# Projecting one row's queries with the weights as the moving operand

## The chip, the cores and the metric

The kernel runs on one core of a Trainium2 chip. Its time is the device time of one execution in microseconds. Before the change three runs gave 1077.71, 1078.51 and 1079.8 us; the median, 1078.51, is what a change is held against. A separate execution was taken with the hardware profiler; all durations below come from it.

## The reference

Two layers, each of an attention block "A" and an MLP block "B", are applied twice to eight rows x of 448 numbers, with the same weights and caches both times. The first A is called pass 0 below, the second pass 1.

```
def A(x):                       # B=8, Sq=1, D=448, Hq=16, Hkv=8, Sk=4096, Dh=256
    q = (x @ wq) in 16 heads of 256
    k, v = k_cache, v_cache, each head used by 2 heads of q
    p = softmax(q k / 16)
    return (p v, heads side by side) @ wo
def B(x):
    h  = gelu(layernorm(x) @ w1)
    x1 = x + shifted(h) @ w2    # shifts by 1 and 2 along a sequence of length 1
    return x1 + gelu(layernorm(x1) @ w3) @ w4

x = x + A(layernorm(x)); x = x + B(layernorm(x))
x = x + A(layernorm(x)); x = x + B(layernorm(x))
```

The sequence has one position, so all four shifts leave zeros and the product with w2 is zero: w1 and w2 drop out of the work. What is large are the two caches: 8 elements x 8 heads x 4096 x 256 in bf16, 134 MB each, and both passes need both.

## The kernel before, in words

**Staging.** One SBUF tile, `places`, holds 15 pieces of 1 MB. A piece is a quarter of the K or the V of two heads of one element. All weights stay in SBUF: `wq_sb` (the first 384 rows of wq as three blocks of 128 rows, the last 64 rows as two halves stacked in one block), `w3_sb`, `wo_sb`, `w4_sb`. For each element, 12 of its 32 pieces are kept from pass 0 to pass 1, so they are loaded once; one more is put aside in PSUM (`away`, `back`), and a quarter of another.

**Order.** The whole order of the work is made when the program is built. `block` and `first_kept` write a list of items (task, K or V, quarter); a task is (pass, element, pair of head pairs). The main loop (L985) walks the list. A K item is turned by DVE (`transpose_k`, L803) and multiplied with the queries (`scores`, L818) into the PSUM bank `sc`, from which ACT takes exponentials (`exps`, L827) into `p_n`. A V item is multiplied with the probabilities by `pv` (L871), 16 products of 256 columns, each with 8 columns of `ptw` as weights, four of them going to the four row groups of the bank `o`. Behind each item `emit_loads` issues on SP's queue the loads for which places have come free; a load waits until the last reader of its place is done. SP's queue thus follows the pace at which items are consumed.

**Generators.** Work that is not tied to an item (finishing an element's heads, the output projection, the MLP, the next queries) is written as generators. `step` (L930) advances them by one `yield` at a time between items, or, for V items of the set `narrow`, between the two halves of an item (`between` in `pv`, at y == 8). A yield of 0 in such a calm stretch runs straight on to the next yield; a yield of 2 or 3 may skip the next turn.

**The chain of one element** (`chain`, L522) runs in pass 0 once the second half of an element's heads is there: `half` (scales the outputs and turns them to columns; it copies a bank of `o` to `o_sb`, and `locked` keeps two such halves apart), the output projection by `wo_sb` (`add_cols`), the MLP (`mlp`: `norm`, w3, gelu, w4), and the queries for pass 1: `project_q(b, 1, ...)`. All of it stands among the V items of `narrow`, which are loaded in halves of 512 KB (`halved`, L793). At the end `give_q` spreads the queries with four products (`spread_q`, L353) and four DVE copies into `qbd`, which the scores of pass 1 use as weights.

**The projection of one element** (L323 to L344). For each of 32 blocks of 128 columns of wq there are four products, one for each block of rows: the 128x128 block of wq is loaded as weights, and x, one column broadcast to 32 (`wide`, L167), streams past. The result comes out in columns, as the queries are wanted, in a region of the bank `misc`. A yield stands behind 32 products, so there are four groups of 32, each followed by half a V item or a whole one. DVE then copies 128x32 values to `qT`.

The eight elements' projections stand at about 172, 300, 429, 558, 675, 784, 893 and 1002 us of the profiled span.

Of the kernel before, what the change touches and what calls it, by code (L numbers as in the profile page):

```python
# [8 lines left out]
FP32 = mybir.dt.float32  # L9
BF16 = mybir.dt.bfloat16  # L10
# [7 lines left out]
def kernel(  # L18
# [27 lines left out]
    nc = tc.nc  # L46
# [3 lines left out]
    Dh = A_k_cache.shape[3]  # L50
    HD = A_wq.shape[1]
    Hq = HD // Dh
# [5 lines left out]
    HC = F // 128  # L58
# [11 lines left out]
    consts = ctx.enter_context(tc.tile_pool(name="consts", bufs=1))  # L70
    work = ctx.enter_context(tc.tile_pool(name="work", bufs=2))
    chn = ctx.enter_context(tc.tile_pool(name="chn", bufs=1))
# [10 lines left out]
    MID = Bn // 2  # L83
# [5 lines left out]
    ident = spare[1][:, 0:256].bitcast(FP32)  # L89
# [1 line left out]
    identb = consts.tile([128, 128], BF16, name="identb")  # L91
    nc.vector.tensor_copy(identb[:], ident)

    usel = consts.tile([128, 4], FP32, name="usel")
    for u in range(2):
        nc.vector.tensor_reduce(
            usel[:, 2 * u : 2 * u + 2],
# [10 lines left out]
        ALU.add,  # L108
    )

    ptz = consts.tile([128, 264], BF16, name="ptw")
    nc.vector.memset(ptz[:], 0.0)
    ptw = ptz[:, 0:256].rearrange("p (r n w) -> p r n w", r=2, w=8)
    psv_t = consts.tile([128, NP * 128], BF16, name="psv")
    psv = [
# [1 line left out]
        for k in range(NP)  # L117
    ]

    misc = psum.tile([128, 512], FP32, name="misc")  # L120
    ot_bank = misc[:, 256:288]
    sc = psum.tile([128, 512], FP32, name="sc")
# [7 lines left out]
    def room_ps(what, nb):  # L130

        at, n = {"y": (288, 8), "st": (296, 2), "h": (298, HC), "q": (288, NB2)}[what]
        if nb == 1:
            return misc[:, at : at + n]
        if nb < Bn:
            at = {"y": 352, "st": 384, "h": 400}[what]
            return misc[:, at : at + n * nb]
        at, n = {"y": (0, 8), "st": (64, 2), "h": (80, HC), "q": (256, NB2)}[what]
        return store[0][:, at : at + n * nb]
# [39 lines left out]
    def xbs(nb):  # L179
        return xb[1] if nb == 1 else xb[Bn][:, :, :nb]  # L180
# [10 lines left out]
    wq_sb = split_tile(HD, "wq_sb")  # L191
# [205 lines left out]
    def mlp_hidden(b0, nb):  # L397

        yield from norm(xT[:, :, b0 : b0 + nb], nb, True)
        h_ps = room_ps("h", nb)  # L400
        for c in range(HC):
            for fc in range(4):
                w, xi = wblk(w3_sb, F, c, fc)
                if nb == 1:
                    wide(h_ps[:, c : c + 1], w, xbs(1)[:, xi, :], fc == 0, fc == 3)
                    continue
                nc.tensor.matmul(
                    h_ps[:, c * nb : c * nb + nb],
                    w,
                    xbs(nb)[:, xi, :],  # L410
                    start=(fc == 0),
                    stop=(fc == 3),
                )
            if c % 7 == 6:
                yield 0 if c == HC - 1 else None
        g_t = chn.tile([128, HC * MID], FP32, tag="g")
        hh = g_t[:, 0 : HC * nb]
        g0 = g_t[:, HC : 2 * HC] if nb == 1 else misc[:, 456 : 456 + HC * nb]
        if nb == 1:
            HT_t = chn.tile([128, HC, 1], BF16, tag="HT")  # L420
            HT = HT_t[:]
        else:
            HT = HTw[:, :, b0 : b0 + nb]

        nc.vector.tensor_scalar_mul(hh, h_ps, 0.5)
        nc.vector.scalar_tensor_tensor(g0, hh, 4 * 0.044715, hh, ALU.mult, ALU.mult)
        nc.vector.scalar_tensor_tensor(g0, g0, 1.0, hh, ALU.add, ALU.mult)
        nc.scalar.activation(g0, g0, ACT.Tanh, scale=2 * 0.7978845608028654)
        yield 0
        nc.vector.scalar_tensor_tensor(  # L430
            HT,
            g0.rearrange("p (c b) -> p c b", b=nb),
            1.0,
            hh.rearrange("p (c b) -> p c b", b=nb),
            ALU.add,
            ALU.mult,
        )
        yield 2
        return HT

    def mlp(b0, nb):
        HT = yield from mlp_hidden(b0, nb)
        yield from out_cols(lambda c: HT[:, c, :], w4_sb, HC, b0, nb, 2)

    def z_cols(zall, gps):

        np_ = len(gps)
        zm = chn.tile([128, 4, np_], FP32, tag=f"zm{np_}")
        zs_t = chn.tile([128, 2], FP32, tag="zs")
        zs = zs_t[:, 0:np_]  # L450
        nc.vector.tensor_add(
            zs, zall[:, 0, gps[0] : gps[-1] + 1], zall[:, 1, gps[0] : gps[-1] + 1]
        )
        nc.vector.tensor_tensor(
            zm[:],
            zs.unsqueeze(1).to_broadcast([128, 4, np_]),
            usel[:].unsqueeze(2).to_broadcast([128, 4, np_]),
            ALU.mult,
        )
        yield  # L460
        z_ps = misc[:, 392 : 392 + 4 * np_].rearrange("p (n g) -> p n g", n=4)
        nc.tensor.matmul(z_ps, ones, zm[:], start=True, stop=True)  # L462
        yield 0
        rz = chn.tile([128, 4, np_], FP32, tag=f"rz{np_}")
        nc.vector.reciprocal(rz[:], z_ps)  # L465
        return rz
# [6 lines left out]
                OT[:, j, h0 : h0 + 2], o_ps[:, j, h0 : h0 + 2], rz[:, 2 * u : 2 * u + 2, 0]  # L473
            )

    def half(o_ps, zall, gps, OT, ready):

        while locked:
            yield
        locked.append(gps)  # L480
        rz = yield from z_cols(zall, gps)

        g8, n8 = gps[0] // 2, 4 * len(gps)
        R_t = chn.tile([128, 8], FP32, tag="R")
        R = R_t[:, 0:n8]
        f0 = 4 * (gps[0] % 2)
        nc.vector.tensor_mul(
            R.rearrange("p (g n) -> p g n", n=4),
            rz[:].rearrange("p n g -> p g n"),
            fold[:, f0 : f0 + n8].rearrange("p (g n) -> p g n", n=4),  # L490
        )
        while not ready():
            yield
        o_sb = chn.tile([128, Dh], FP32, tag="o_sb")
        nc.scalar.copy(o_sb[:], o_ps)  # L495
        yield
        nc.vector.memset(o_ps, 0.0)  # L497
        free_o.append(o_ps)
        ot_ps = ot_bank[:, 16 * g8 : 16 * g8 + 2 * n8].rearrange("p (j h) -> p j h", j=2)
        for j in range(2):  # L500
            nc.tensor.matmul(  # L501
                ot_ps[:, j], o_sb[:].rearrange("p (i j) -> p j i", j=2)[:, j], R, start=True, stop=True
            )
        yield 0
        nc.vector.tensor_copy(OT, ot_ps)  # L505
        locked.pop()
        yield

    locked = []
    free_o = list(o_banks)  # L510

    def first_half(b, st, ready):
# [6 lines left out]
        xs = xT[:, :, b : b + 1]  # L519
        nc.vector.tensor_add(xs, xs, y_room(1)[:, 0])  # L520

    def chain(b, st, ready):  # L522
        OT = work.tile([128, 2, Hq // 2, 1], BF16, tag="OTb", bufs=1)
        yield from half(st["o", 1], st["z"], [2, 3], OT[:, :, :, 0], ready)
        yield from add_cols(
            y_room(1)[:, 1],
            lambda i: OT[:, i % 2, i // 2 - Hq // 2],
            wo_sb,
            range(NB2 // 2, NB2),
            2,  # L530
        )
        xs = xT[:, :, b : b + 1]
        nc.vector.tensor_add(xs, xs, y_room(1)[:, 1])
        yield from mlp(b, 1)
        qT = chn.tile([128, NB2], BF16, tag="qT2", bufs=2)
        yield from project_q(b, 1, qT[:].unsqueeze(2))
        state[1, b] = {"qT": qT}
        give_q((1, b))

# [381 lines left out]
    gens, pairs_done, p_of = [], {}, {}  # L921
# [63 lines left out]
    for idx, it in enumerate(items):  # L985
# [7 lines left out]
        n, kv, c = it  # L993
        ps, b, gp = tasks[n]
# [4 lines left out]
        p = where[(b, gp), (kv, c)] if kept_now else where[it]  # L999
# [3 lines left out]
        if kv == 0:  # L1003
# [6 lines left out]
            st = state[ps, b]  # L1010
# [13 lines left out]
            x = c - c % 2  # L1024
# [11 lines left out]
                    scores(two[0], x, qbd, gp, between=turn)  # L1036
                    scores(two[1], x + 1, qbd, gp)
            if c == 1:
                p_n = work.tile([128, 4, 32, 4], BF16, tag="p_sb", bufs=1)
                p_of[n] = p_n  # L1040
            if c % 2 == 1:
                exps(p_of[n], st["z"], gp, c // 2)
                if kept_now and c == 3:
# [4 lines left out]
        else:  # L1048
            st = state[ps, b]
# [28 lines left out]
            else:  # L1078
# [9 lines left out]
                if c == 0 and (alone_now or pairs_done.get((ps, b), 0) % 2 == 1):  # L1088
# [5 lines left out]
                    if ps == 0:  # L1094
                        g = (first_half if done == 2 else chain)(b, st, ready)
# [100 lines left out]
```

## Time and profile before

| | |
|---|---|
| median of three runs | 1078.51 us |
| profiled execution | 1078.9 us |
| its span | 1077.1 us |
| mean granted TensorE clock | 0.663 |
| read from HBM | 436.28 MB |
| rate over the span | 405 GB/s |
| products by wq in the eight chains (L170) | 1024, mean 184 ns each, 33.5 us busy in all |
| their weight loads | 1024, 30.0 us busy |
| halves of V (512 KB loads) | 202, median 7.4 us from issue to landing |

A line of a group names the source line, engine and operation, then the output tile, the inputs, the shapes and the count. "PE" is TensorE's matmuls, "PEld" its weight loads, which run beside matmuls; "SPq" is the queue on which SP issues loads. In a timeline a line stands for consecutive instructions of one kind: start and length in us, and in brackets how long the engine had been idle before, and what ended that. The windows view gives, for a stretch, the busy time of each engine with the number of instructions, the granted clock, the busy share of the 16 DMA engines and the rate in GB/s. The chain of waits goes back from the last instruction to whatever released each step.

### The profile page before, as it was taken

The numbers are of one execution on the slowest core, as the hardware profiler recorded it, in microseconds if no ns is written. First come the engines' busy times: TensorE is split into PE (matmuls) and PEld (weight loads), VectorE is DVE, ScalarE is ACT, GpSimd is POOL, SyncE is SP. The second block draws the span as 40 slices with busy tenths as digits, with TensorE's granted clock in tenths as the row PEclk, the third lists the DMA queues.
The fourth block names the chain that finished last, engine by engine and source line by source line (L and its number), as shares of the span: only waits on it lengthen the run. The fifth ranks groups of instructions, "written<-read, shape, count | busy, mean of one in ns | idle before, by whom it ended". The sixth has DMA issues, their size and how long they took to land.

```text
span 1077.1 us, 29813 instructions
## 1 busy us (share of the span) xinstructions
PE 631.0 (59%) x13292; PEld 399.4 (37%) x13292; DVE 610.7 (57%) x1266; ACT 162.0 (15%) x612; POOL 16.4 (2%) x27
## 2 busy tenths in 40 slices
PE   3244457644765447654586547754775467756775
PEld 2122225422443224432254324532453245433554
DVE  4357841677426872368724773297439743875371
ACT  0001111111111111111111111111111111111110
POOL 0000000000000000000000000000000000000000
PEclk9998568755686556865567656755585567656765
DMA  9999999999999999999999999999999999999994
GB/s 359 394 426 423 426 412 402 424 424 423 403 404 425 426 422 389 417 425 424 420 385 417 424 424 401 397 426 426 409 399 424 424 410 402 425 424 389 409 419 176
DMA packets 69200, 438.22 MB, mean 407 GB/s; under 512 B 7368, under 2 KB 11344, under 8 KB 38736
## 3 DMA queue, kind: packets, MB, share of 16 engines
q1 hardware_dynamic: 68880, 435.94, 98.7%
q8 instruction: 104, 1.70, 0.6%
q10 hardware_dynamic: 192, 0.38, 0.1%
q14 instruction: 24, 0.20, 0.0%
HBM read 436.28 MB, written 0.01 MB: 405 GB/s over the span
## 4 chain that ended last, share of the span: by engine, by line
DMA 64%; PE 18%; DVE 11%; SPq 3%; issue 2%; ACT 2%; POOL 0%; DVEq 0%; ACTq 0%
DMA places<-in_A_v_cache_dram 35%; DMA places<-in_A_k_cache_dram 28%; DVE places L803 7%; PE o L871 6%; PE sc L818 6%; PE misc L170 3%; SPq L189 2%; PE misc L501 1%; SPq L790 1%; ACT p_n L827 1%; DMA wq_sb<-in_A_wq_dram 1%; DVE places L845 1%; DVE store L838 1%; DVE qbd L357 0%; PE misc L854 0%
## 5 line engine op out<-in xcount | busy, mean ns | idle before, releaser
L803 DVE STREAM_TRANSPOSE places<-places 128x512 uint32<-128x512 uint32 (+1 forms) x576 | 457.9, 857 | 127.0 <-DMA places<-in_A_k_cache_dram 125.5
L818 PE MATMUL sc<-places,qbd 128*8 128x256 bf16 (+1 forms) x4896 | 239.8, 343 | 247.8 <-DVE places L803 241.5
L871 PE MATMUL o<-places,ptw 128*8 128x256 bf16 x3968 | 232.4, 360 | 130.7 <-DMA places<-in_A_v_cache_dram 106.1
L818 PEld LDWEIGHTS <-qbd 128*8 128x8 bf16 x4896 | 125.9, 101 | 325.1 <-DVE places L803 147.1
L871 PEld LDWEIGHTS <-ptw 128*8 128x8 bf16 x3968 | 97.9, 99 | 195.5 <-issue 122.1
L827 ACT ACTIVATE p_n<-sc 128x256 bf16<-128x256 f32 x128 | 95.2, 743 | 382.1 <-PE sc L818 382.1
L981 ACT COPY ptw<-psv 128x32 bf16<-128x32 bf16 x248 | 52.6, 227 | 196.4 <-PE o L871 190.5
L861 ACT CAST psv<-misc 128x128 bf16<-128x128 f32 x64 | 17.0, 266 | 237.0 <-PE misc L854 237.0
L465 DVE RECIPROCAL rz<-misc 128x8 f32<-128x8 f32 (+1 forms) x35 | 6.6, 190 | 70.6 <-PE misc L462 70.6
L357 DVE CAST qbd<-misc 32x64 bf16<-32x64 f32 x104 | 22.4, 215 | 29.9 <-PE misc L353 28.9
L170 PEld LDWEIGHTS <-wq_sb 128*128 128x128 bf16 x1024 | 30.0, 101 | 15.2 <-issue 14.7
L170 PE MATMUL misc<-xb,wq_sb 128*128 128x32 bf16 x1024 | 33.5, 184 | 3.6 <-issue 2.9
L501 PE MATMUL misc<-R_t,o_sb 128*128 128x8 f32 (+1 forms) x132 | 26.7, 311 | 13.4 <-ACT o_sb L495 7.1
L170 PEld LDWEIGHTS <-wo_sb 128*128 128x128 bf16 x1024 | 30.1, 102 | 10.9 <-issue 10.7
L170 PE MATMUL misc<-OT,wo_sb 128*128 128x32 bf16 x1024 | 32.7, 185 | 1.9 <-DVE OT L505 1.7
L827 ACT ACTIVATION_READ_ACCUMULATOR p_n<-sc 128x1 f32 x128 | 33.8, 264 | 0.0
L501 PEld LDWEIGHTS misc<-R_t,o_sb 128*128 128x128 f32 x132 | 23.8, 252 | 23.5 <-ACT o_sb L495 13.6
L170 PEld LDWEIGHTS <-w_sb 128*128 128x128 bf16 x896 | 27.3, 103 | 13.8 <-issue 13.2
L343 DVE CAST qT<-misc 128x32 bf16<-128x32 f32 x8 | 1.5, 192 | 50.8 <-PE misc L170 50.8
L269 POOL TENSOR_TENSOR t<-t,nhalf 128x2 f32<-128x2 f32 (+2 forms) x20 | 14.0, 705 | 1048.4 <-DVE t L290 1048.4
L497 DVE MEMSET o<- 128x256 f32 x33 | 9.0, 272 | 34.2 <-PE o L871 31.2
L854 PEld LDWEIGHTS <-p_n 128*128 128x128 bf16 x256 | 11.8, 105 | 31.7 <-issue 20.4
(111 smaller groups left out, 312.3 us busy)
## 6 DMA issues: line engine op xcount, KB each, us to landing
places<-in_A_k_cache_dram SPq DMA_DIRECT2D x65, 2048.0 KB, 19.1
places<-in_A_v_cache_dram SPq DMA_DIRECT2D x107, 1024.0 KB, 21.0
places<-in_A_v_cache_dram SPq DMA_DIRECT2D x202, 512.0 KB, 7.4
places<-in_A_k_cache_dram SPq DMA_DIRECT2D x62, 1024.0 KB, 13.2
places<-in_A_v_cache_dram SPq DMA_DIRECT2D x8, 768.0 KB, 14.3
wo_sb<-in_A_wo_dram SPq DMA_DIRECT2D x1, 3584.0 KB, 27.1
wq_sb<-in_A_wq_dram SPq DMA_DIRECT2D x3, 1024.0 KB, 9.9
w_sb<-in_B_w_dram SPq DMA_DIRECT2D x1, 1568.0 KB
```

The costliest lines, as they stand in the source:

```text
L170: nc.tensor.matmul(bass.AP(out.tensor, out.offset, [out.ap[0], (1, WIDE)]), w, x.to_broadcast([128, WIDE]), start=start, stop=stop, skip_g ...
L189: nc.sync.dma_start(t[:, fc * cols : (fc + 1) * cols], src[fc * 128 : fc * 128 + 128, :])
L269: nc.gpsimd.tensor_tensor(rs[:, k0:k1].rearrange("p n b -> p (n b)"), ve[:, k0:k1].rearrange("p n b -> p (n b)"), nhalf[:].to_broadcast([1 ...
L357: nc.vector.tensor_copy(qbd[32 * a : 32 * a + 32, :, :, a, :], qs.rearrange("p e (f g u h) -> p (e f) u g h", f=2, u=2, h=2)[:, :, u],)
L501: nc.tensor.matmul(ot_ps[:, j], o_sb[:].rearrange("p (i j) -> p j i", j=2)[:, j], R, start=True, stop=True)
L803: nc.vector.transpose(w, w)
L818: nc.tensor.matmul(sc[32 * k : 32 * k + 8, 128 * x : 128 * (x + nx)], qbd[:, ep, gp].rearrange("p a h -> p (a h)"), v, start=(n == 0), sto ...
L827: nc.scalar.activation(p_sb[:, :, :, 2 * u : 2 * u + 2].rearrange("p t i x -> p x t i"), sc[:, 256 * u : 256 * u + 256].rearrange("p (x t ...
L854: nc.tensor.matmul(pt_ps[:, t], p_sb[:, t].rearrange("p i x -> p (i x)"), cols, start=True, stop=True,)
L861: nc.scalar.copy(p_to, pt_ps.rearrange("p t k (a h) -> p a (t k) h", a=4))
L871: nc.tensor.matmul(o_ps[32 * q : 32 * q + 8, :], ptz[:, at : at + 8], v[:, y * Dh : (y + 1) * Dh], start=False, stop=(y >= 12), skip_group ...
L981: nc.scalar.copy(ptw[:, ring_of[it], :, 6:8], psv[slot_of[it[0]]][:, it[2]])
```

## The change

The projection of one element is done the other way round. The column x, broadcast to 8 columns, is loaded as weights, and wq streams past it in rows of 512 columns. A result row appears eight times over in a row group of the PSUM bank `sc`, at partitions 32q to 32q+7. Four row groups take four blocks of 512 columns at a time, and four products (one for each block of rows of wq) add up in each: 16 products make 2048 of the 4096 queries. DVE copies the bank `sc` (128x512) to bf16 in `rows`, then the same is done for the other 2048. Eight products then turn the rows to columns: 128x128 of `rows` are the weights, and `pickb`, 128x4 with a one at partitions 0, 32, 64 and 96, selects the first row of each row group. DVE copies the 128x32 columns to `qT` as before.

The room for `rows` is a new tile `buf`, 128x512 in fp32. It takes the place of the two tiles that held `o_sb` and `p_n`; both are now halves of `buf`. As `rows` covers them, the chain holds the lock of `half` (`hold=True`) until the queries are turned. `pick` and `pickb` are made once at the start, in widened tiles that were there. The gelu is split off from `mlp_hidden` into a function with the same instructions.

The yields of the new code give three steps among the halves of V in place of four groups: 16 products, 16 products, 8 turning products, each followed by half a V item. The four products of `spread_q` come behind the third such half; before, they came behind the fifth half after the first group (the fourth, for elements 4 to 7).

```diff
-        qT = chn.tile([128, NB2], BF16, tag="qT2", bufs=2)
-        yield from project_q(b, 1, qT[:].unsqueeze(2))
+
+        yield from norm(xs, 1, False)
+        q_ps = room_ps("q", 1)
+        for ph in range(2):
+            for fc in range(4):
+                for q in range(4):
+                    at = (fc * HD if fc < 3 else 3 * HD - 2048 * ph) + 512 * (4 * ph + q)
+                    row(q, fc if fc < 3 else 4 - ph, wq_sb[:, at : at + 512], fc)
+            yield 0
+            nc.vector.tensor_copy(rows[:, 512 * ph : 512 * ph + 512], sc[:])
+            yield
+        for ph in range(2):
+            for k in range(4):
+                c = (k % 2) * Hq + 8 * ph + k // 2
+                nc.tensor.matmul(
+                    q_ps[:, c : c + 7 : 2],
+                    rows[:, 512 * ph + 128 * k : 512 * ph + 128 * k + 128],
+                    pickb,
+                    start=True,
+                    stop=True,
+                )
+        yield 0
+        locked.pop()
+        qT = chn.tile([128, NB2], BF16, tag="qT2", bufs=2)
+        nc.vector.tensor_copy(qT[:], q_ps)
+        yield
...
+    rows = buf[:].bitcast(BF16)
+
+    def row(q, xi, w, fc):
+
+        n = w.shape[-1]
+        nc.tensor.matmul(
+            sc[32 * q : 32 * q + 8, 0:n],
+            xbs(1)[:, xi, :].to_broadcast([128, 8]),
+            w,
+            start=fc == 0,
+            stop=fc == 3,
+            skip_group_check=True,
+        )
...
-        yield from half(st["o", 1], st["z"], [2, 3], OT[:, :, :, 0], ready)
+        yield from half(st["o", 1], st["z"], [2, 3], OT[:, :, :, 0], ready, hold=True)
...
+    buf = consts.tile([128, 2 * Dh], FP32, name="buf")
...
-        o_sb = chn.tile([128, Dh], FP32, tag="o_sb")
-        nc.scalar.copy(o_sb[:], o_ps)
+        o_sb = buf[:, 0:Dh]
+        nc.scalar.copy(o_sb, o_ps)
...
-        locked.pop()
+        if not hold:
+            locked.pop()
...
-                p_n = work.tile([128, 4, 32, 4], BF16, tag="p_sb", bufs=1)
-                p_of[n] = p_n
+                p_of[n] = buf[:, Dh:].bitcast(BF16).rearrange("p (t i x) -> p t i x", t=4, i=32)
```

More of the change, by code (lines that the diff above doesn't have):

```diff
@@ L92 @@
     nc.vector.tensor_copy(identb[:], ident)
-    usel = consts.tile([128, 4], FP32, name="usel")
+    usel_t = consts.tile([128, 8], FP32, name="usel")
+    usel, pick = usel_t[:, 0:4], usel_t[:, 4:8]
     for u in range(2):
@@ L109 @@
     )
-    ptz = consts.tile([128, 264], BF16, name="ptw")
-    nc.vector.memset(ptz[:], 0.0)
+    nc.vector.tensor_copy(pick, ident.rearrange("p (q r) -> p q r", q=4)[:, :, 0])
+    ptz = consts.tile([128, 268], BF16, name="ptw")
+    nc.vector.memset(ptz[:, 0:264], 0.0)
+    pickb = ptz[:, 264:268]
+    nc.vector.tensor_copy(pickb, pick)
     ptw = ptz[:, 0:256].rearrange("p (r n w) -> p r n w", r=2, w=8)
@@ L415, in mlp_hidden @@
                 yield 0 if c == HC - 1 else None
-        g_t = chn.tile([128, HC * MID], FP32, tag="g")
-        hh = g_t[:, 0 : HC * nb]
-        g0 = g_t[:, HC : 2 * HC] if nb == 1 else misc[:, 456 : 456 + HC * nb]
         if nb == 1:
@@ L423, in mlp_hidden, with gelu @@
             HT = HTw[:, :, b0 : b0 + nb]
+        yield from gelu(h_ps, HC, nb, HT)
+        return HT
+    def gelu(h_ps, n, nb, HT):
+        g_t = chn.tile([128, HC * MID], FP32, tag="g")
+        hh = g_t[:, 0 : n * nb]
+        g0 = g_t[:, n : 2 * n] if nb == 1 else misc[:, 456 : 456 + n * nb]
         nc.vector.tensor_scalar_mul(hh, h_ps, 0.5)
@@ L438, in mlp_hidden @@
         yield 2
-        return HT
     def mlp(b0, nb):
@@ L456, in z_cols @@
             zs.unsqueeze(1).to_broadcast([128, 4, np_]),
-            usel[:].unsqueeze(2).to_broadcast([128, 4, np_]),
+            usel.unsqueeze(2).to_broadcast([128, 4, np_]),
             ALU.mult,
@@ L474, in scale_o, with half @@
             )
-    def half(o_ps, zall, gps, OT, ready):
+    def half(o_ps, zall, gps, OT, ready, hold=False):
         while locked:
@@ L501, in half @@
             nc.tensor.matmul(
-                ot_ps[:, j], o_sb[:].rearrange("p (i j) -> p j i", j=2)[:, j], R, start=True, stop=True
+                ot_ps[:, j], o_sb.rearrange("p (i j) -> p j i", j=2)[:, j], R, start=True, stop=True
             )
```

## The prediction

> **What bounds the kernel now.** I read the page from the top: busy shares, slices, DMA queues, chain. Then the busy table of the eight stretches that the change touches, the TensorE timeline inside two of them, and what SP's queue waits for.
>
> ```profile
> span 1077.1 us, 29813 instructions
> PE 631.0 (59%) x13292; PEld 399.4 (37%) x13292; DVE 610.7 (57%) x1266; ACT 162.0 (15%) x612; POOL 16.4 (2%) x27
> ...
> DMA  9999999999999999999999999999999999999994
> ...
> q1 hardware_dynamic: 68880, 435.94, 98.7%
> q8 instruction: 104, 1.70, 0.6%
> ...
> DMA 64%; PE 18%; DVE 11%; SPq 3%; issue 2%; ACT 2%; POOL 0%; DVEq 0%; ACTq 0%
> ```
>
> No engine is busy over 59%. The DMA engines are full in all slices but the last, 98.7% of their time goes to the data queue, and DMA is 64% of the chain of waits. The time is the caches' bytes at the rate at which they flow, with a tail in the last slice in which the changed code no longer runs. So the change can move the time in two ways: by bytes it takes off the DMA engines, or by making the queue run short of free places while it runs.
>
> The eight stretches (8 us each, from just before a projection of one element's queries by wq until its q is spread; the first row is a stretch of the same loads ahead of one):
>
> ```profile
> 152.00:160.00 8.00, 6.10 (x134) 3.91 (x127) 1.16 (x7) 1.15 (x5) 0.00 (x0) 0.77 1.02 409
> 172.00:180.00 8.00, 6.66 (x180) 4.58 (x173) 0.64 (x4) 0.66 (x3) 0.00 (x0) 0.79 1.02 390
> 300.00:308.00 8.00, 7.13 (x180) 4.83 (x180) 0.45 (x3) 0.67 (x3) 0.00 (x0) 0.63 1.02 407
> ```
>
> Columns: length, busy PE, PEld, DVE, ACT, POOL, granted clock, DMA share, GB/s. PE is nearly full here, DVE nearly empty, DMA still full. The other six give 412, 391, 402, 404, 392 and 409 GB/s; the mean of all eight is 400.9. Against the 409 of the first row that is 64 us x 8.1/409 = 1.3 us of DMA throughput lost in all eight.
>
> TensorE in the second (element 1) and the sixth (element 5):
>
> ```profile
> 300.02 0.60 PE L871 MATMUL o<-places,ptw 128*8 128x256 bf16 x8 [0.88 <-DMA places<-in_A_v_cache_dram]
> 300.55 1.06 PE L170 MATMUL misc<-xb,wq_sb 128*128 128x32 bf16 x32
> 301.54 0.60 PE L871 MATMUL o<-places,ptw 128*8 128x256 bf16 x8
> ...
> 307.27 0.39 PE L871 MATMUL o<-places,ptw 128*8 128x256 bf16 x8 [0.39 <-DMA places<-in_A_v_cache_dram]
> 307.49 0.25 PE L353 MATMUL misc<-qT,identb 128*32 128x32 bf16 x4
> ...
> 310.21 1.92 PE L818 MATMUL sc<-places,qbd 128*8 128x256 bf16 x32
> ```
> ```profile
> 783.41 0.39 PE L871 MATMUL o<-places,ptw 128*8 128x256 bf16 x8 [0.78 <-DMA places<-in_A_v_cache_dram]
> ...
> 790.29 0.37 PE L170 MATMUL misc<-xb,wq_sb 128*128 128x32 bf16 x8 [1.16 <-issue]
> 790.59 0.60 PE L871 MATMUL o<-places,ptw 128*8 128x256 bf16 x8
> ...
> 792.34 0.60 PE L871 MATMUL o<-places,ptw 128*8 128x256 bf16 x8 [0.20 <-DMA places<-in_A_v_cache_dram]
> ```
>
> Each L871 group of 8 takes half a V piece (512 KB); where it waits for DMA, the halves come 1.27 us apart (298.75, 300.02). Four wq groups of 32 products, 1.06 to 0.97 us each, stand between them. The 0.60 of an L871 group is the low clock, 0.39 the high one.
>
> ```profile
> SPq L793 <- PE o L871: 114.0, 141, 2.5
> ```
>
> This is the loop to watch: SP issues the next half only when an L871 group has freed a place. A late group makes a late issue.
>
> **The change part by part.** The order of all other instructions on PE, ACT, DVE, POOL and SP stays as it was; only the eight stages differ.
>
> *Instructions fetched.* A stage had 128 products and 128 weight loads; it gets 32 + 8 of each: 256 - 80 = 176 fewer, 1408 in all. 2 x 13292 over 104 packets is 256 PE instructions a packet, so 5.5 packets go. A packet costs 0.6% x 1077.1 / 104 = 0.062 us of all 16 engines (1.0 us of one): -0.34 us.
> The Trainium skill, "Runtime: NRT & Kernel Launch", section "Instruction fetch mechanics", has these blocks of 256 instructions and calls their cost mostly hidden. The trace agrees on the size, but shows them on the engines that bound the kernel; by the page this term would be 0 and the sum 0.34 us higher.
>
> *Loss now in the stages.* A packet holds up one of 16 engines by 1 us while a piece needs all 16. PE instructions in a stage with its six L871 groups go from about 360 to 184, roughly half. The gain is between 0 (the loss has another cause) and all 1.3 us; I take half, -0.6.
>
> *PE in the stage.* Removed: 4 groups, 4.0 to 4.2 us, with an L871 group or two behind each. Added: two blocks of 16 products with 512 columns, four at a time beside each other as L871 and L818 are. A block streams as many columns as the L818 row of 32 x 256: 1.92 us at the low clock (310.21), 1.10 at the high one (901.63). Then eight products of 4 columns, by the row of four L854 products (0.29) about 0.3 us.
>
> *DVE copies of sc.* Two of 128x512 f32 to bf16. Nearest rows: L343 128x256 in 0.425 us and 128x32 in 0.192, a line that gives 0.69 us; bounds are 0.49 (memset of sc, 128x512) and 0.85 (twice 0.425). Block 2 waits for copy 1, the last four turning products for copy 2. Queued behind those waits on PE are the L871 groups and so SP's issues. On DVE nothing useful stands behind: it is busy 0.45 of 8 us here.
>
> *Walk at the low clock* (0 = 300.55; halves at 0.74, 2.01, 3.28, 4.55, 5.82). Block 1 until 1.9; L871 at 1.9, late by 1.2; copy 1 until 2.65; block 2 from 2.7 to 4.6; L871 at 4.6, late by 2.6; copy 2 until 5.35; turning until 5.6; L871 at 5.6, late by 2.3; then the spread of q, 6.4 (late 1.85), 6.95 (1.1), 7.5 and even. At the high clock throughout, the second group is late by 0.8; with block 1 low and block 2 high, by 1.75. Now the lateness is 0.25 to 0.5 as a rule.
>
> *What lateness costs.* Element 5 shows it: the 1.16 us stall made a group run at 790.59 that was due at 783.41 + 4 x 1.27 = 788.49, 2.1 us late, and at 792.34 the loop was back on its beat (783.41 + 7 x 1.27 = 792.30). Free. Element 4 has a stall of 1.29, is 2.26 late, and slips by 0.47 (683.69 against 674.33 + 8.89). So the cover, V halves already issued, holds for about 2.1 us. At 2.6 the price lies between 0 and 0.47 + 0.5 = 1.0 us a stage. In these stages the high clock comes 2.7 to 4.9 us after the start (6.7 in element 1), that is, during block 2 or after it. I take half of the stages late by over 2.1, at element 4's 0.4: +1.6; ends 0 and +8.
> The Trainium skill, "TensorE: Matmul & The Clock Gate", Part 1, says the clock doubles after about 3.4 us of sustained work, in a window that runs free. The eight stages agree within its scatter; by 3.4 us block 2 would end near 4.1, the lateness be 2.1 and this term nothing.
>
> *Costed at nothing.* The earlier q: no score waits for it now, since L871 groups that wait for DMA stand between (308.56). Lock held to the stage's end, o_sb and p_n in one buffer, gelu split off: no instruction moves. Two 128x4 copies at the start, 0.2 us each, are behind the wq load (PE waits 10.2 us for it); without that cover they cost 0.4. The first score after a stage needs sc copied: done two L871 groups earlier.
>
> *Sum.* -0.34 - 0.6 + 1.6 = +0.7 us on the profiled 1078.9 (span 1077.1 and 1.8 around it): 1079.6. That execution is 0.4 above the median of 1078.51, so 1079.2 for a median.
>
> **The rivals.** About 0.2%, 2.2 us, is what a measurement here can tell from no change.
>
> 1. *The queue runs short (slower).* In the narrow stretches both blocks meet the low clock, places come free 2.6 us late, SP issues too late and the DMA engines idle. Price 1.0 us a stage at most, 8.0 - 0.9 = +7.1: 1085.6; halfway, 1082. It decides from 0.4 us a stage. For: PE is 7.13 of 8 busy at clock 0.63 in element 1. Against: element 5.
>
> 2. *Fetches were the loss (faster).* Compared with the beat of 1.27, V after the stages comes late by 0.58, 0.90, 0.46, 1.30, 0.47, 0.04, 0.11 and 0.53 us, 4.4 in all. If fetches made this, half goes, with the 0.34: -2.5, 1076.0; all of it, 1073.8. The three issue stalls (1.29, 1.16, 0.49) speak for it. Against: the bytes lost are only 1.3 us' worth.
>
> 3. *All lateness stays in the cover.* Without the +1.6 the sum is -0.9: 1077.6. For: element 5; an early high clock would do it. Against: element 4. It is told from no change no better than the forecast, and shares its chance.
> The Trainium skill's clock rule above leads to this case.
>
> **How the numbers follow.** No change that can be told (the forecast's sum, or rival 3): 0.50, time 1079.2, own range 1076.4 to 1080.7. Rival 1: 0.29. Rival 2: 0.21. The range reaches half of rival 2 and most of rival 1: 1075.6 to 1084.
>
> **What would show it.** In the changed profile: q8 at about 98 or 99 packets; DMA slices all 9; the new blocks at 1.1 to 1.9 us; L871 groups behind block 2 without a DMA wait and 1 to 2.6 us late; the eight stretches at 400 GB/s or a little more. Rival 1 would show as stretches under 390 GB/s; rival 2 as 407 or more and no issue stalls. I am wrong if the copies take far over 0.7 us, if block 2 never meets the high clock, or if the order of the queue outside the stages shifts.

## The result and the profile after

The median went from 1079.59 us (1077.27 to 1082.55, 15 runs) to 1084.61 us (1081.81 to 1091.23, 15 runs): a ratio of 1.0048, with a 95% interval of 1.0035 to 1.0062. The change costs about 5 us. The forecast was 1079.2 us, most likely no change that can be told; the rival that came true is the first, "the queue runs short".

The profiled execution after is the longest of its 15 runs, 1091.23 us, while the one before was an ordinary one (1078.9). So the profile after is read for the place of the loss and the medians for its amount.

The page after, with the rows that answer to those shown of before:

```profile
span 1089.4 us, 28430 instructions
PE 636.5 (58%) x12588; PEld 385.7 (35%) x12588; DVE 621.0 (57%) x1284; ACT 161.8 (15%) x612; POOL 16.3 (2%) x27
...
DMA  9999999999999999999999999999999999999994
...
q1 hardware_dynamic: 68880, 435.94, 98.3%
q8 instruction: 98, 1.61, 0.6%
...
DMA 60%; PE 19%; DVE 14%; SPq 3%; issue 2%; ACT 1%; POOL 0%; DVEq 0%; ACTq 0%
```

This page shows almost nothing. The caches' bytes are the same, 435.94 MB; no engine is busy over 58%; the DMA row still reads 9 in 39 slices, for a slice of 27 us hides a stretch of six. What has moved is the chain: less of it on DMA (60% after 64%), more on PE and DVE. The loss is seen only at the rate of the loads in narrow stretches.

The windows view, columns as in the prediction (length, busy PE, PEld, DVE, ACT, POOL, granted clock, DMA share, GB/s). Each row is the stretch from 6 to 12 us *after* an element's projection has begun. Elements 0 to 2 and 5 before:

```profile
178.20:184.20 6.00, 3.56 (x100) 2.60 (x103) 1.38 (x7) 0.99 (x4) 0.00 (x0) 1.00 1.04 417
306.60:312.60 6.00, 3.91 (x88) 2.60 (x84) 1.38 (x7) 0.64 (x2) 0.00 (x0) 0.72 1.01 395
435.40:441.40 6.00, 3.93 (x93) 2.63 (x93) 1.38 (x7) 0.99 (x4) 0.00 (x0) 0.80 1.02 406
790.00:796.00 6.00, 5.26 (x120) 3.65 (x124) 1.38 (x7) 0.99 (x4) 0.00 (x0) 0.72 1.01 367
```

The same four elements after:

```profile
179.40:185.40 6.00, 3.71 (x76) 2.37 (x76) 1.19 (x6) 1.21 (x5) 0.00 (x0) 0.72 0.88 283
309.50:315.50 6.00, 3.71 (x76) 2.20 (x75) 1.19 (x6) 1.21 (x5) 0.00 (x0) 0.72 0.90 309
439.50:445.50 6.00, 3.69 (x76) 2.19 (x71) 1.19 (x6) 1.21 (x5) 0.00 (x0) 0.72 0.83 257
...
799.60:805.60 6.00, 2.67 (x80) 1.79 (x76) 1.22 (x6) 1.23 (x5) 0.00 (x0) 0.99 0.93 323
```

The mean of all eight is 395 GB/s before and 297 after. Eight stretches of 6 us at 297 in place of 395 lose 48 x 98 / 395 = 11.9 us; the two profiled spans differ by 12.3. So nearly all of the loss stands in these stretches. In the stretch 0 to 6 us, in which the projection itself runs, the mean is 400 before and 388 after; in the 6 us ahead of it 402 and 383, from 12 to 18 us 404 and 416. Each of these is worth 1.4 to 2.3 us, and not all in one direction, so such a sum is good to about 2 us.

TensorE in element 1 after (start, length, and in brackets idle time and what ended it):

```profile
303.08 0.60 PE L918 MATMUL o<-places,ptw 128*8 128x256 bf16 x8 [0.67 <-DMA places<-in_A_v_cache_dram]
303.46 1.92 PE L536 MATMUL sc<-wq_sb,xb 128*8 128x512 bf16 x16
305.17 0.64 PE L918 MATMUL o<-places,ptw 128*8 128x256 bf16 x8
306.18 1.88 PE L536 MATMUL sc<-wq_sb,xb 128*8 128x512 bf16 x16 [0.37 <-DVE buf L567]
307.84 0.55 PE L918 MATMUL o<-places,ptw 128*8 128x256 bf16 x8
...
310.66 0.39 PE L918 MATMUL o<-places,ptw 128*8 128x256 bf16 x8 [0.57 <-DMA places<-in_A_v_cache_dram]
...
314.00 0.64 PE L918 MATMUL o<-places,ptw 128*8 128x256 bf16 x8
317.48 0.39 PE L918 MATMUL o<-places,ptw 128*8 128x256 bf16 x8 [2.84 <-DMA places<-in_A_v_cache_dram]
```

L918 is the product of V with the probabilities (L871 before). Against a beat of 1.27 us from 303.08, the group at 305.17 is 0.82 late and the one at 307.84 is 2.22 late. At 310.66 the halves are on the beat again (303.08 + 6 x 1.27 = 310.70), as the prediction had read it in element 5. But each of these groups frees a place. From the last group ahead of the projection on, SP issued its halves at 303.7, 305.9, 308.4, 309.5, 309.9 and 310.4; before, in the same element, at 300.7, 302.2, 303.7, 304.5, 306.0 and 307.7. The third is thus issued 5.0 us after the start of the projection in place of 3.2. What was issued late is missed one landing time (7.3 us in the median) later: TensorE waits 2.84 us for V up to 317.48, for the half that was issued at 309.5 and took 8.0 us to land.

The transfers themselves, in slices of 0.5 us. The DMA view of element 1, first before (297.1 to 317.1), then after (300 to 320); in both the projection begins at the end of the seventh slice:

```profile
DMA  9999999999999999999999999999998999998899
GB/s 434 393 418 401 393 418 410 434 418 410 393 401 410 434 401 426 410 369 385 410 418 410 426 401 393 426 401 434 360 352 311 451 410 426 401 311 328 377 393 410
```
```profile
DMA  9999999999999999999999978897898999999999
GB/s 328 401 393 401 410 434 418 418 393 377 369 352 426 459 377 377 418 418 401 369 336 401 377 279 287 279 303 270 262 295 246 328 393 418 336 434 401 401 426 442
```

After, the rate swings about 400 up to 311.5 us and is 246 to 303 in the eight slices from there to 315.5, 8 to 12 us behind the start of the projection. The DMA share falls less, to 0.7 to 0.9.

The two groups that were priced in the prediction:

```profile
L536 PE MATMUL sc<-wq_sb,xb 128*8 128x512 bf16 x256 | 29.1, 604 | 4.4 <-DVE buf L567 2.9
...
L567 DVE CAST buf<-sc 128x512 bf16<-128x512 f32 x16 | 11.1, 691 | 31.4 <-PE sc L536 31.4
```

The new blocks keep TensorE busy for 29.1 us in all, where the products they replace took 33.5; a copy takes 0.691 us, and TensorE waits 0.37 us or so for each first one.

### The profile page after: what moved, and what is told of

The parts are those of the page before. It is cut to its first block, busy times and chain, and to the rows that moved or that the text cites. A ratio compares the mean times of both kernels' runs of the same rounds, so it can differ in the third digit from the quotient of the medians.

```text
span 1089.4 us, 28430 instructions
## 1 busy us (share of the span) xinstructions
PE 636.5 (58%) x12588; PEld 385.7 (35%) x12588; DVE 621.0 (57%) x1284; ACT 161.8 (15%) x612; POOL 16.3 (2%) x27
## 3 DMA queue, kind: packets, MB, share of 16 engines
q1 hardware_dynamic: 68880, 435.94, 98.3%
## 4 chain that ended last, share of the span: by engine, by line
DMA 60%; PE 19%; DVE 14%; SPq 3%; issue 2%; ACT 1%; POOL 0%; DVEq 0%; ACTq 0%
DMA places<-in_A_v_cache_dram 35%; DMA places<-in_A_k_cache_dram 24%; DVE places L850 9%; PE o L918 6%; PE sc L865 5%; PE sc L536 3%; PE misc L175 2%; SPq L194 2%; DVE store L885 1%; DVE buf L567 1%; SPq L837 1%; PE misc L509 1%; DMA wq_sb<-in_A_wq_dram 1%; ACT buf L874 1%; POOL t L274 0%
## 5 line engine op out<-in xcount | busy, mean ns | idle before, releaser
L865 PE MATMUL sc<-places,qbd 128*8 128x256 bf16 (+1 forms) x4896 | 245.4, 349 | 246.2 <-DVE places L850 239.2
L918 PE MATMUL o<-places,ptw 128*8 128x256 bf16 x3968 | 234.9, 364 | 133.9 <-DMA places<-in_A_v_cache_dram 110.8
L918 PEld LDWEIGHTS <-ptw 128*8 128x8 bf16 x3968 | 100.9, 101 | 208.1 <-issue 132.7
L874 ACT ACTIVATE buf<-sc 128x256 bf16<-128x256 f32 x128 | 95.0, 742 | 397.5 <-PE sc L865 397.5
L509 PE MATMUL misc<-R_t,buf 128*128 128x8 f32 (+1 forms) x132 | 27.8, 320 | 12.8 <-ACT buf L503 7.1
L874 ACT ACTIVATION_READ_ACCUMULATOR buf<-sc 128x1 f32 x128 | 33.8, 264 | 0.0
L509 PEld LDWEIGHTS misc<-R_t,buf 128*128 128x128 f32 x132 | 24.9, 263 | 23.9 <-ACT buf L503 15.4
L536 PE MATMUL sc<-wq_sb,xb 128*8 128x512 bf16 x256 | 29.1, 604 | 4.4 <-DVE buf L567 2.9
L567 DVE CAST buf<-sc 128x512 bf16<-128x512 f32 x16 | 11.1, 691 | 31.4 <-PE sc L536 31.4
L901 PE MATMUL misc<-identb,buf 128*128 128x32 bf16 x256 | 18.2, 191 | 9.0 <-ACT buf L874 7.3
L901 PEld LDWEIGHTS <-buf 128*128 128x128 bf16 x256 | 11.7, 105 | 32.9 <-issue 21.0
## 6 DMA issues: line engine op xcount, KB each, us to landing
places<-in_A_v_cache_dram SPq DMA_DIRECT2D x8, 768.0 KB, 14.8
```

Source lines behind the costliest of these rows:

```text
L509: nc.tensor.matmul(ot_ps[:, j], o_sb.rearrange("p (i j) -> p j i", j=2)[:, j], R, start=True, stop=True)
L536: nc.tensor.matmul(sc[32 * q : 32 * q + 8, 0:n], xbs(1)[:, xi, :].to_broadcast([128, 8]), w, start=fc == 0, stop=fc == 3, skip_group_check ...
L567: nc.vector.tensor_copy(rows[:, 512 * ph : 512 * ph + 512], sc[:])
L865: nc.tensor.matmul(sc[32 * k : 32 * k + 8, 128 * x : 128 * (x + nx)], qbd[:, ep, gp].rearrange("p a h -> p (a h)"), v, start=(n == 0), sto ...
L874: nc.scalar.activation(p_sb[:, :, :, 2 * u : 2 * u + 2].rearrange("p t i x -> p x t i"), sc[:, 256 * u : 256 * u + 256].rearrange("p (x t ...
L901: nc.tensor.matmul(pt_ps[:, t], p_sb[:, t].rearrange("p i x -> p (i x)"), cols, start=True, stop=True,)
```

## The experiments

**Theories.** T, the theory after seeing the profile: the same work, gathered in two blocks of 16 with only half a V item behind each, frees places late, and the loads issued late are lost to the DMA engines. Rivals: R, the streamed rows as such (their shape, their copies); S, the rest of the change (the shared buffer, the lock held longer, the gelu split off); C, the low clock that the scores behind the stage then meet.

The table gives the medians and the ratios to the kernel before, whose median in the three series of runs was 1079.3 to 1079.9, and from the profiled executions the mean rate from 6 to 12 us behind the start of the projection (before 395).

| run | median, us (runs) | ratio (interval) | GB/s |
|---|---|---|---|
| after | 1084.61 (15) | 1.0048 (1.0035 to 1.0062) | 297 |
| e11_again (the same kernel) | 1086.60 (6) | 1.0076 (1.0049 to 1.0102) | 334 |
| e1_split | 1079.28 (11) | 0.9995 (0.9983 to 1.0007) | 410 |
| e2_spaced | 1080.51 (11) | 1.0010 (0.9996 to 1.0024) | 383 |
| e3_shell | 1079.59 (11) | 1.0001 (0.9991 to 1.0011) | 387 |
| e4_dense_old | 1089.05 (4) | 1.0095 (1.0079 to 1.0110) | 314 |
| e5_once_more | 1085.47 (7) | 1.0050 (1.0033 to 1.0068) | 339 |
| e6_twice_more | 1095.68 (4) | 1.0140 (1.0116 to 1.0165) | 279 |
| e7_late_start | 1082.08 (12) | 1.0021 (1.0005 to 1.0036) | 379 |
| e8_two_copies | 1086.36 (10) | 1.0064 (1.0045 to 1.0083) | 314 |
| e9_less | 1078.30 (12) | 0.9985 (0.9973 to 0.9997) | 404 |
| e10_fine | 1078.86 (12) | 0.9993 (0.9982 to 1.0003) | 401 |

The ratios come with their intervals from the comparison of the runs and differ a little from the quotients of the medians.

**The streamed rows, cut finer.** The changed kernel with one more yield in the middle of each block:

```diff
                 for q in range(4):
                     at = (fc * HD if fc < 3 else 3 * HD - 2048 * ph) + 512 * (4 * ph + q)
                     row(q, fc if fc < 3 else 4 - ph, wq_sb[:, at : at + 512], fc)
+                if fc == 1:
+                    yield
```

> The changed kernel with each block of 16 row products cut into two steps of 8, so that half a V item stands between them: the same instructions, four steps of about 0.95 us instead of two of 1.9. Theory (crowding: too much TensorE work between two V halves, places come free 2 us late and the DMA engines run short 7 us later): the lateness falls to under 1 us and the time comes back to 1079 us, within 2 us of the kernel before. Rival (the streamed rows themselves: their clock, their reads of SBUF, the copies and the waits on them): it stays at 1083 to 1086.

Measured: 1079.28 us, the time of the kernel before. Every instruction of the change is there; only half a V item now stands between two blocks of 8. Its element 1 on TensorE (here L920 is the product with V):

```profile
301.98 1.07 PE L536 MATMUL sc<-wq_sb,xb 128*8 128x512 bf16 x8
302.89 0.60 PE L920 MATMUL o<-places,ptw 128*8 128x256 bf16 x8
303.27 1.07 PE L536 MATMUL sc<-wq_sb,xb 128*8 128x512 bf16 x8
304.17 0.60 PE L920 MATMUL o<-places,ptw 128*8 128x256 bf16 x8
305.13 0.81 PE L536 MATMUL sc<-wq_sb,xb 128*8 128x512 bf16 x8 [0.36 <-DVE buf L569]
```

The wait of 0.36 us for the copy is still there and costs nothing that can be measured. The first four V groups come late by 0.23, 0.30, 0.60 and 0.51 us (mean of the eight elements), against 1.03, 2.32, 2.24 and 1.36 in the profile after. The rate holds 410 GB/s. R falls: neither the shape nor the copies cost anything by themselves that can be measured.

**More V behind each block.** The changed kernel, with two halves of V in place of one after each copy:

```diff
             nc.vector.tensor_copy(rows[:, 512 * ph : 512 * ph + 512], sc[:])
-            yield
+            yield 2
```

> The changed kernel with its blocks of 16 left whole, but two V halves instead of one behind each block and its copy. Crowding: each block still makes the next half about 0.8 to 1.2 us late, but the second block no longer adds to it; 1079 to 1082. If the copies and the waits on them were the cost, they are covered here by another half, and it comes out at 1079 as well; if the length of one block were the cost, it stays at 1083 or more.

Measured: 1080.51, ratio 1.0010 (0.9996 to 1.0024). The blocks stay 16 long and still make the first group 0.92 us late, but the second is late by only 0.34. Most of the loss is gone; a rest of 1 us can be neither shown nor excluded. Two blocks close together cost more than the blocks by themselves.

**All but the projection.** The changed kernel with the old projection in its place; the buffer, the lock and the gelu stay as changed:

```diff
-        yield from norm(xs, 1, False)
-        q_ps = room_ps("q", 1)
-        for ph in range(2):
...
-        yield 0
+        qT = chn.tile([128, NB2], BF16, tag="qT2", bufs=2)
+        yield from project_q(b, 1, qT[:].unsqueeze(2))
         locked.pop()
-        qT = chn.tile([128, NB2], BF16, tag="qT2", bufs=2)
-        nc.vector.tensor_copy(qT[:], q_ps)
-        yield
```

> The changed kernel with the old projection by 128 products put back, the rest of the change kept: one buffer for the output copy and the probabilities, the lock held to the end of the projection, gelu split off, the selection made at the start. Theory: as before, ratio 0.999 to 1.001. Rival (the shared buffer or the lock costs): above 1.002.

Measured: 1079.59, ratio 1.0001 (0.9991 to 1.0011). S falls.

**The old products, gathered.** The kernel before with its four groups of 32 joined to two of 64:

```diff
-                if h % 8 == 7:
-                    yield (3, 0)[j] if h == Hq - 1 else None
+                if h == Hq - 1:
+                    yield (None, 0)[j]
```

> The kernel before with its four groups of 32 products joined to two of 64, so that no streamed row, copy or turning is there, but the TensorE work stands as crowded as in the change: two steps of 2.1 us with one V half between. Crowding: lateness of 2.5 us and 3 to 7 us more than before, 1083 to 1087. Rival (streamed rows and copies are the cost): as before, within 1.5 us.

Measured: 1089.05, +9.2 us against the median of before in that series (by the ratio 10.3): there are no streamed rows and no copies of `sc` here, and the loss is there all the same, larger than expected. Element 1 on TensorE:

```profile
304.11 1.91 PE L170 MATMUL misc<-xb,wq_sb 128*128 128x32 bf16 x64
305.94 0.60 PE L871 MATMUL o<-places,ptw 128*8 128x256 bf16 x8
306.47 1.89 PE L170 MATMUL misc<-xb,wq_sb 128*128 128x32 bf16 x64
308.30 0.39 PE L871 MATMUL o<-places,ptw 128*8 128x256 bf16 x8
```

The blocks have the length of the streamed ones. V comes late by 1.09, 2.18, 1.70 and 0.67 us. Eight stretches at 314 in place of 395 GB/s lose 9.8 us; the span is 10.5 longer. Together with e1_split this settles T against R in both directions: old products gathered lose, new ones cut finer do not. Why this kernel's median lies 4 us above that of the change at about the same lateness is open; in the profiled executions, of which that of the change is its longest and this one is near its median, the two are near each other (1089.4 and 1087.6 us of span).

**What a microsecond of TensorE costs there.** The kernel before with its first group of 32 products done twice, then three times: 1.0 and 1.9 us more of TensorE's time per stage, the order otherwise unchanged.

```diff
-                for fc in range(4):
+                again = 2 if nb == 1 and j == 0 and h < 8 else 1
+                for fc in list(range(4)) * again:
```

In e6_twice_more the 2 is a 3.

> The kernel before with the first group of 32 products of each stage done twice: 1.0 us more TensorE work in one place per stage, nothing else. It makes the next halves of V 1 to 1.8 us late. The prediction's price (a cover of about 2.1 us, free below it): 0 to 1 us more, 1079 to 1080.5. Theory now (lateness is paid one landing time later, from about 1 us on): 2 to 3 us more, 1081.5 to 1083.

> The same group done three times: 1.9 us more in one place, lateness 2.3 to 2.9 us, like that of the change, without rows, copies or turning. The prediction's price: 0.4 to 1.0 us a stage, 1083 to 1088. Theory now: 6 to 9 us more, 1085.5 to 1089. If the streamed rows or the copies were a cost of their own, it would stay under the changed kernel's 1084.6 at equal lateness.

Measured: 1085.47 and 1095.68, +6.15 and +16.4 us against 1079.32 (by the ratios 5.4 and 15.1): 0.7 to 0.8 us a stage for 1.0 us of work, 1.9 to 2.0 us a stage for 1.9. Both are far above the prediction's price and above what T then expected. Two of the eight stretches from 6 to 12 us of e5_once_more, elements 1 and 4:

```profile
309.30:315.30 6.00, 4.58 (x136) 3.09 (x136) 1.38 (x7) 1.00 (x4) 0.00 (x0) 1.00 0.99 317
...
683.91:689.91 6.00, 5.37 (x136) 3.91 (x140) 1.41 (x7) 1.22 (x5) 0.00 (x0) 0.70 0.78 266
```

The eight lose 48 x 56 / 395 = 6.8 us by their mean of 339; the span grew by 6.4. In e6_twice_more they lose 14.1 us by their mean of 279, of 20.6 by which the span grew.

How late one group comes does not set the price alone. The second V group is as late in e6_twice_more as in the change (2.34 and 2.32 us), at three times the loss. What differs is how long V stays late: over the first seven groups of a stage the lateness adds up to 14.8 us in e6_twice_more, 8.2 in e5_once_more, 7.6 in the change and 4.3 before. e4_dense_old, with 6.2, does not fit this order, and why is open.

**The opposite: less work in the stage.** The kernel before, with only the first of four products for half of the columns, so that its queries are incomplete (three quarters of the products of the second half are left out, 1.5 us a stage):

```diff
-                for fc in range(4):
+                short = nb == 1 and j == 1
+                for fc in range(1 if short else 4):
...
-                        wide(q_ps[:, j * Hq + h, :], w, xbs(1)[:, xi, :], fc == 0, fc == 3)
+                        wide(q_ps[:, j * Hq + h, :], w, xbs(1)[:, xi, :], fc == 0, short or fc == 3)
```

> The kernel before with three of the four products left out for each of the last 64 products of a stage (the second half of every head's queries is computed from the first 128 rows alone, so the output is not the reference's): the groups are 32, 32, 8 and 8, TensorE has 1.5 us less work per stage. Theory (each us of TensorE work among these halves is paid about 0.8 to 1 to one, there is no free cover): some of the 1.0 us that the DMA engines lose around a stage comes back, 2 to 5 us less, 1075 to 1077.5. If the stage before the change was already free of crowding (work below some level costs nothing): 0 to 1 us less.

Measured: 1078.30, ratio 0.9985 (0.9973 to 0.9997): -1.6 us in all, 0.2 a stage: less than T expected (2 to 5) and more than its alternative, no crowding left before the change (0 to 1). So the price has a knee, and the kernel before stands near it: the next 1.0 us of work costs 0.7 to 0.8 us a stage, the last 1.5 us cost 0.2. In this profile the first scores behind the stage run at the low clock (1.93 us for 32) in seven of eight stages, and still its median is the lowest of all: by itself that low clock costs nothing, and C falls as the cause. Whether it adds to the loss where V is late already is not settled. In the profile after, the three elements whose first scores met the high clock kept 327 GB/s and the five others 279; in e11_again, the same kernel, elements 3 and 6 met the high clock at 328 and 257 GB/s, and element 4 the low one at 411.

**The stage two halves of V later.** The changed kernel with two more yields ahead of the blocks, meant to move the stage against the scores that follow:

```diff
         q_ps = room_ps("q", 1)
+        yield
+        yield
         for ph in range(2):
```

> The changed kernel with its two blocks started two V halves later, so that q is spread 16 products before the next scores as it was before the change, not 32. Rival within crowding: the stage ends early, TensorE then waits for V, the clock falls, and the next scores run at 1.92 us in place of 1.1, late for the loop. By it, 1080 to 1082, with the first scores after a stage at 1.1 to 1.5 us. By crowding in the stage alone: no change, 1083.5 to 1086.

Measured: 1082.08, ratio 1.0021 (1.0005 to 1.0036), half of the loss back. The first scores behind the stage ran at the high clock in all eight elements (1.05 to 1.15 us; after, 1.92 to 1.94 in five), which speaks for C, at least as something that adds to the loss. V is also less late here (0.82, 1.88, 1.77, 0.89), and the 1 MB loads that follow the halves are issued sooner, 6.4 to 6.7 us after the start of the projection in place of 8.6 to 9.2. Which of these gives the half back is argued, not shown.

**The copy shared by two engines.** The changed kernel, each copy of `sc` split into 256 columns on DVE and 256 on ACT, to shorten TensorE's wait:

```diff
-            nc.vector.tensor_copy(rows[:, 512 * ph : 512 * ph + 512], sc[:])
+            nc.vector.tensor_copy(rows[:, 512 * ph : 512 * ph + 256], sc[:, 0:256])
+            nc.scalar.copy(rows[:, 512 * ph + 256 : 512 * ph + 512], sc[:, 256:512])
```

> The changed kernel with each copy of sc shared between two engines, DVE the first 256 columns and ACT the others, side by side: the waits behind block 1 and for the last four turning products shrink by 0.25 to 0.3 us each, so the second half is 2.0 us late in place of 2.25. Crowding: 1 to 2 us less than the changed kernel, 1082.5 to 1084. If the waits on the copies were the main cost: 1080 to 1081. If they are no cost: 1084 to 1085.5.

Measured: 1086.36, ratio 1.0064 (1.0045 to 1.0083), no gain. The edit did not do what it was meant to:

```profile
306.63 0.43 DVE L567 CAST buf<-sc 128x256 bf16<-128x256 f32 x1 [2.16 <-PE sc L536]
307.09 0.37 ACT L568 CAST buf<-sc 128x256 bf16<-128x256 f32 x1 [2.21 <-DVE buf L567]
```

ACT's half waited for DVE's, and 0.43 + 0.37 us one after the other is more than the 0.69 of one copy. The Trainium skill, "PSUM — Partial Sum Buffer", section "Terms", says that no two engines may be at the same bank and quadrant of PSUM at once; both copies read the bank `sc`, and the trace shows them one after the other, though not whether the bank or the shared `buf` made it so. On the price of the copy wait this run says nothing.

**Finer still.** The changed kernel in steps of 4, 4, 8, 8 and 8 products:

```diff
+                if fc == 1 or (ph == 0 and fc == 0):
+                    yield
```

> The changed kernel with its row products in steps of 4, 4, 8, 8 and 8, each followed by a half: one step more than in the run that cut each block in two. Crowding: 1077.5 to 1079.5, no worse than that run. If q now comes too late for the first scores behind it (one half stands between, not two): 1080 to 1082.

Measured: 1078.86, ratio 0.9993 (0.9982 to 1.0003). It is level with the kernel before and with e1_split; no version here beats the kernel before by more than can be told.

**The changed kernel once more, in a later series.**

> The changed kernel itself, for a second profile beside these two: 1083 to 1086, ratio 1.003 to 1.007, with the loss again 6 to 12 us behind the start of each stage.

Measured: 1086.60 (1082.98 to 1093.14), ratio 1.0076 (1.0049 to 1.0102): slower again, and its profiled execution again its longest. Here the stretches from 6 to 12 us (334 GB/s) account for 48 x 61 / 395 = 7.4 of the 14.2 us by which its span exceeds the one before, and the six microseconds ahead of the projection, those in it and those from 12 to 18 (397, 393 and 395 GB/s against 402, 400 and 404) for 48 x (5 + 7 + 9) / 395 = 2.6 more. The rest was not placed.

This profile, in which the eight stages differ more than in the first, shows the price of lateness within one kernel. Where the second V group came 0.6 us late, the rate from 6 to 12 us was 411 GB/s; at 1.4 to 1.6 us late it was 362 to 387, at 1.9 us 328, at 2.2 us 254 and 303, and at 2.9 us 257.

## Why the prediction was wrong, point by point

*What bounds the kernel, and the two ways in which the change can act: right.* The bytes stayed, and the queue ran short.

*Instructions fetched: right in count, not told in time.* 98 packets after 104, as worked out (98 or 99). The 0.34 us are below what the runs tell.

*Loss now in the stages (-0.6): not confirmed.* If fetches had made it, e1_split, which has all of the change's shorter code, should show some of it. It gives -0.5 us, with an interval from -1.8 to +0.8: neither shown nor excluded. Rival 2 (-2.5 and -4.7) is excluded for e1_split at both of its prices.

*PE in the stage, the copies, and the walk: right.* Blocks of 1.92 and 1.88 us against 1.92, copies of 0.691 against 0.69. In the profile the groups behind block 1, behind block 2 and behind the turning came 1.03, 2.32 and 2.24 us late against 1.2, 2.6 and 2.3. Block 2 met the low clock in six of eight elements (1.85 to 1.88 us; 1.25 and 1.54 in elements 4 and 7), where half had been taken. The Trainium skill's rule ("TensorE: Matmul & The Clock Gate", Part 1: about 3.4 us of sustained work) gave the estimate that block 2 ends 4.1 us after the start; in element 1 the trace has it at low speed until 308.06, 4.6 us after the start. The same part says that the window runs free, and the spread over the elements agrees with that: in the profile after, the granted clock rises 3.2 to 6.1 us after the start of the projection. The prediction had the eight stages of before agree with the rule within its scatter. There the granted clock rises 2.8 to 4.0 us after the start in seven elements, but 5.3 us after it in element 1 (at 305.88; the prediction's 6.7 is the next fast group of V), so one of the eight lies well outside.

*What lateness costs: this is the step that failed.* The prediction put it: "So the cover, V halves already issued, holds for about 2.1 us", with element 5 before as its witness: back on the beat at 792.34, hence "Free". That looked for the price at the next arrivals, which were loads issued *before* the group was late. The loads that it delayed land a landing time later, 7.3 us, and there the price stood. The trace of before had a sign of it: the stretch 790 to 796 us ran at 367 GB/s where the other seven mean 399, which is 6 x 32 / 399 = 0.5 us lost. That this one hole is the price of that one delay is argued and not shown: its lowest half-microseconds, 295 to 319 GB/s, stand at 793 to 794.5 us, 4.5 to 6 us after the group was due and so sooner than a landing time. That there is no free cover of 2.1 us is shown by e5_once_more: in six of its eight stages no V group was more than about 2.0 us late, and from 6 to 12 us these six ran at 354 GB/s, where the same six elements had 398 before. The term was taken as +1.6 us, 0.4 in half of the stages; in the profile after, the second group was over 2.1 us late in seven of the eight. With the +5.0 measured and the 0 to 0.9 of gains that may stand against it, it measured 5 to 6 us, 0.6 to 0.7 us in each of eight stages; e5_once_more gives 0.7 to 0.8 a stage for 1.0 us of added work. The end of the range given for it (+8) held it.

*Costed at nothing: right.* e3_shell shows buffer, lock and gelu at 1.0001 (0.9991 to 1.0011); the copies' waits are covered in e1_split.

*Rival 1: right in its mechanism and its sign, underrated in its chance, its place a little off.* Its price "from 0.4 us a stage" was passed, its mark of stretches under 390 GB/s is there, but 6 to 12 us behind the start rather than in the stretches that were named. Element 5 was held against it, while element 5's stretch was the slowest of the eight before.

## What to carry to other kernels

Where a load is issued when its consumer frees a place, judge a delay by the rate of the transfers over the next landing time or so (here the holes stood 4 to 10 us behind the group that was late), and not by whether the next piece arrives on time: that piece was issued before the delay. With the DMA engines nearly full, work added at one place of the consumer's loop cost 0.7 to 1 us for each us here, though no engine was busy over 60%. The same work cut into steps as short as the beat of the loads cost nothing here, so look at the largest step between two consumers before looking at the count of instructions or their busy time.

## What was not expected of the hardware

The rate falls more than the share of the DMA engines. In element 1 after it is 309 GB/s at a share of 0.90, against 395 at 1.01 before: 12% less for each unit of share. Loads were not lacking altogether either: at 312 us four halves were issued and had not landed (308.4, 309.5, 309.9, 310.4), where a landing time of 7.7 us and a beat of 1.27 keep six outstanding before. Four sixths of 418 GB/s are 279, and the slices there show 246 to 303. That the rate goes with the number of outstanding loads is a reading of this one hole and was not tested. The count alone does not give it: with landing times of about 7 us, only four were out at 309 us too (issued at 302.5, 303.7, 305.9 and 308.4), and the slices from 308.5 to 309.5 us read 418 and 401.

The half issued at 308.4, into the thinned queue, landed after 4.7 us, and one issued in the burst behind it after 8.0; before, all in that element took 7.4 to 7.9.

The profiled execution was the longest of all runs of the kernel in the change (twice), in e6_twice_more (1099.61) and in e8_two_copies (1090.64), but not in e4_dense_old, e5_once_more or the kernels that keep the beat. Why is open. A profile of one execution overstated the loss of the change, 12 us against 5.
